# Linear attention and a swish layer on one core: a hand-ordered kernel with one chunk per batch, row tiles and DMA transposes

## The chip, the cores and the metric

The kernel runs on one core of a Trainium2 chip. A core has five engines with queues of their own: PE (TensorE, matmuls; PEld is its weight load), DVE (VectorE), ACT (ScalarE), POOL (GpSimd) and SP (SyncE, which here only issues DMAs). The metric is the device time of one execution in microseconds. Each engine works through its own instructions in order; where one needs what another engine made, it waits on a semaphore, and everything behind it on its engine waits too.

## What is computed

A linear attention over 8 batches and 8 heads, 576 tokens of 64 numbers each, gives x, one row of 512 numbers a token. Then comes a two-layer network with a swish in the middle.

```
q, k, v: (8, 8, 576, 64) float32; w_in (512, 2048); w_out (2048, 512); beta (2048)

q_s = exp(q - max(q, axis=-1));  q_s = q_s / (sum(q_s, axis=-1) + 1e-09)
k_s = exp(k - max(k, axis=2));   k_s = k_s / (sum(k_s, axis=2) + 1e-09)
kv  = einsum('bhsd,bhse->bhde', k_s, v)
att = einsum('bhsd,bhde->bhse', q_s, kv)
x   = att.transpose(0, 2, 1, 3).reshape(4608, 512)
h   = x @ w_in
g   = h * (1.0 / (1.0 + exp(-beta * h)))
out = g @ w_out
```

The softmax of q runs over the 64 numbers of a token, that of k over the 576 tokens of a head. Inputs and output are float32 in HBM; both kernels multiply in bf16. Both also write the swish as h/2 * (1 + tanh(beta h/2)), with the half folded into the cast of w_out.

## The kernel before

A scheduling layer (a tile framework) takes the program as written and puts each engine's instructions in an order of its own, by dependences and free buffers. So attention of one batch, and matmuls of another, stand mixed on PE.

`attention(b)` (called for b = 0 to 7) works on one batch in five pieces of tokens, 128, 128, 128, 128 and 64 rows. For every piece it loads q on SP's queue (L109), k on POOL's (L115) and v on POOL's, cast to bf16 on the way (L121). A row of a head is 64 float32, so each packet is 256 bytes. ACT takes exp of q (L129) and of k (L146), without subtracting a maximum. DVE sums q over each head (L131), takes the reciprocal (L135) and multiplies (L137). Then, for each of four pairs of heads, PE adds up kvE over the five pieces (L157); a column of ones beside v gives the sum over k, and DVE divides by it (L167 to L173). PE transposes the normalised q of the pair against an identity (L179), DVE copies the result out of PSUM (L185), and PE multiplies q by kv, two 64 x 64 tiles of the array at once (L193, L199). ACT copies x, transposed, into `xT` (L205). `xT` is cut into nine chunks of 512 tokens, which don't fall together with the batches of 576.

`mlp_A(c)` goes over 16 blocks of 128 hidden features of one chunk: four matmuls of 512 columns (L213) into a PSUM bank, tanh on ACT (L221), one DVE operation that makes g (L225). `mlp_B(c)` makes four output blocks of 128 tokens, 16 matmuls of 512 columns each (L241), a copy on ACT (L249) and a store on SP's queue (L251). There are 576 matmuls of either kind.

The weights come in twelve loads on SP's queue (L74, L80) behind the first q loads, and DVE casts them to bf16 (L86, L90). The main loop calls attention of batch b, then `mlp_A` of chunk b and `mlp_B` of chunk b - 1.

Of the kernel before, what the change touches and what calls it, by code (L numbers as in the profile page):

```python
# [12 lines left out]
ACTF = mybir.ActivationFunctionType  # L13


@with_exitstack
def kernel(
# [10 lines left out]
    nc = tc.nc  # L28
# [5 lines left out]
    NTOK = B * S  # L34
    KT = DM // P
    NJ = FF // P
    CHUNK = 512
    NCH = NTOK // CHUNK
    assert NTOK % CHUNK == 0
    S_CHUNKS = [(0, 128), (128, 128), (256, 128), (384, 128), (512, 64)]  # L40
    NSC = len(S_CHUNKS)
    HP = H // 2

    const = ctx.enter_context(tc.tile_pool(name="const", bufs=1))
    wst = ctx.enter_context(tc.tile_pool(name="wstage", bufs=2))
    stage = ctx.enter_context(tc.tile_pool(name="stage", bufs=3))
    atn = ctx.enter_context(tc.tile_pool(name="atn", bufs=2))
    xtp = ctx.enter_context(tc.tile_pool(name="xt", bufs=1))
    gt = ctx.enter_context(tc.tile_pool(name="gt", bufs=2 * NJ))
    outp = ctx.enter_context(tc.tile_pool(name="outp", bufs=2))  # L50
    psA = ctx.enter_context(tc.tile_pool(name="psA", bufs=1, space=bass.MemoryType.PSUM))
    psM = ctx.enter_context(tc.tile_pool(name="psM", bufs=2, space=bass.MemoryType.PSUM))

    identity = const.tile([P, P], BF16, name="identity")
    make_identity(nc, identity[:])

    beta_t = const.tile([P, NJ], F32, name="beta_t")
    nc.sync.dma_start(beta_t[:], moe_beta.rearrange("(j p) -> p j", p=P))
    beta_half = const.tile([P, NJ], F32, name="beta_half")
    nc.vector.tensor_single_scalar(beta_half[:], beta_t[:], 0.5, ALU.mult)  # L60

    w_in_b = const.tile([P, KT, FF], BF16, name="w_in_b")
    w_out_b = const.tile([P, NJ, DM], BF16, name="w_out_b")
    w_in_dram = moe_w_in.rearrange("(kt p) f -> p kt f", p=P)
    w_out_dram = moe_w_out.rearrange("(j p) f -> p j f", p=P)

    w_stage_in = []
    w_stage_out = []

    def issue_weight_dmas():  # L70
        for i in range(2 * KT):
            kt, half = divmod(i, 2)
            t = wst.tile([P, FF // 2], F32, tag="wst_in", bufs=4, name=f"w_in_st{i}")
            nc.sync.dma_start(  # L74
                t[:], w_in_dram[:, kt, half * (FF // 2) : (half + 1) * (FF // 2)]
            )
            w_stage_in.append(t)
        for jj in range(NJ // 4):
            t = wst.tile([P, 4, DM], F32, tag="wst_out", bufs=2, name=f"w_out_st{jj}")
            nc.sync.dma_start(t[:], w_out_dram[:, 4 * jj : 4 * jj + 4, :])  # L80
            w_stage_out.append(t)

    def cast_weights():
        for i in range(2 * KT):
            kt, half = divmod(i, 2)
            nc.vector.tensor_copy(  # L86
                w_in_b[:, kt, half * (FF // 2) : (half + 1) * (FF // 2)], w_stage_in[i][:]
            )
        for jj in range(NJ // 4):
            nc.vector.tensor_single_scalar(  # L90
                w_out_b[:, 4 * jj : 4 * jj + 4, :], w_stage_out[jj][:], 0.5, ALU.mult
            )

    xT = [xtp.tile([P, KT, CHUNK], BF16, name=f"xT{c}") for c in range(NCH)]

    gT_chunks: dict[int, list] = {}

    STAGE_BUFS = 3
    ATN_DEEP = 2 * NSC

    def attention(b: int):
        Ek = []
        qs = []
        vaug = []
        q_st = []
        k_st = []
        for ci, (s0, rows) in enumerate(S_CHUNKS):
            qt = stage.tile([P, H, D], F32, tag="q_st", bufs=NSC)
            nc.sync.dma_start(  # L109
                qt[:rows], q[b, :, s0 : s0 + rows, :].rearrange("h p d -> p h d")  # L110
            )
            q_st.append(qt)
        for ci, (s0, rows) in enumerate(S_CHUNKS):
            kt_ = stage.tile([P, H, D], F32, tag="k_st", bufs=NSC)
            nc.gpsimd.dma_start(  # L115
                kt_[:rows], k[b, :, s0 : s0 + rows, :].rearrange("h p d -> p h d")
            )
            k_st.append(kt_)
        for ci, (s0, rows) in enumerate(S_CHUNKS):
            vt = atn.tile([P, H, D + 1], BF16, tag="vaug", bufs=ATN_DEEP)  # L120
            nc.gpsimd.dma_start(  # L121
                vt[:rows, :, 0:D], v[b, :, s0 : s0 + rows, :].rearrange("h p d -> p h d")
            )
            vaug.append(vt)

        for ci, (s0, rows) in enumerate(S_CHUNKS):
            nc.vector.memset(vaug[ci][:rows, :, D : D + 1], 1.0)  # L127
            Eq = atn.tile([P, H, D], BF16, tag="Eq")
            nc.scalar.activation(Eq[:rows], q_st[ci][:rows], ACTF.Exp)  # L129
            qz = atn.tile([P, H], F32, tag="qz")  # L130
            nc.vector.tensor_reduce(  # L131
                qz[:rows], Eq[:rows], axis=mybir.AxisListType.X, op=ALU.add
            )
            rqz = atn.tile([P, H], F32, tag="rqz")
            nc.vector.reciprocal(rqz[:rows], qz[:rows])  # L135
            qst = atn.tile([P, H, D], BF16, tag="qs", bufs=ATN_DEEP)
            nc.vector.tensor_tensor(  # L137
                qst[:rows],
                Eq[:rows],
                rqz[:rows].unsqueeze(2).to_broadcast((rows, H, D)),  # L140
                ALU.mult,
            )
            qs.append(qst)

            Ekt = atn.tile([P, H * D], BF16, tag="Ek", bufs=ATN_DEEP)
            nc.scalar.activation(  # L146
                Ekt[:rows, :],
                k_st[ci][:rows].rearrange("p h d -> p (h d)"),
                ACTF.Exp,
            )  # L150
            Ek.append(Ekt)

        col_abs = b * S
        for j in range(HP):
            kvE = psA.tile([P, 2 * (D + 1)], F32, tag="kvE")
            for ci, (s0, rows) in enumerate(S_CHUNKS):
                nc.tensor.matmul(  # L157
                    kvE[:, :],
                    Ek[ci][:rows, ds(P * j, P)],
                    vaug[ci][:rows].rearrange("p h e -> p (h e)")[  # L160
                        :rows, ds(2 * j * (D + 1), 2 * (D + 1))
                    ],
                    start=(ci == 0),
                    stop=(ci == NSC - 1),
                )
            rkz = atn.tile([P, 1], F32, tag="rkz")
            nc.vector.reciprocal(rkz[0:D, :], kvE[0:D, D : D + 1])  # L167
            nc.vector.reciprocal(rkz[D:P, :], kvE[D:P, 2 * D + 1 : 2 * D + 2])
            kvp = atn.tile([P, D], BF16, tag="kvp")
            nc.vector.tensor_scalar(  # L170
                kvp[0:D, :], kvE[0:D, 0:D], rkz[0:D, :], None, op0=ALU.mult
            )
            nc.vector.tensor_scalar(  # L173
                kvp[D:P, :], kvE[D:P, D + 1 : 2 * D + 1], rkz[D:P, :], None, op0=ALU.mult
            )

            qsT_ps = psA.tile([P, S], BF16, tag="qsT_ps", bufs=2)
            for ci, (s0, rows) in enumerate(S_CHUNKS):
                nc.tensor.transpose(  # L179
                    qsT_ps[:, s0 : s0 + rows],  # L180
                    qs[ci][:rows].rearrange("p h d -> p (h d)")[:rows, ds(j * P, P)],
                    identity[:rows, :rows],
                )
            qsT = atn.tile([P, S], BF16, tag="qsT")
            nc.vector.tensor_copy(qsT[:, :], qsT_ps[:, :])  # L185

            s_done = 0
            while s_done < S:
                c = (col_abs + s_done) // CHUNK
                off = (col_abs + s_done) % CHUNK  # L190
                w = min(CHUNK - off, S - s_done)
                xps = psA.tile([P, CHUNK], F32, tag="xps")
                nc.tensor.matmul(  # L193
                    xps[0:D, 0:w],
                    kvp[0:D, :],
                    qsT[0:D, s_done : s_done + w],
                    tile_position=(0, 0),
                )
                nc.tensor.matmul(  # L199
                    xps[D:P, 0:w],  # L200
                    kvp[D:P, :],
                    qsT[D:P, s_done : s_done + w],
                    tile_position=(64, 64),
                )
                nc.scalar.copy(xT[c][:, j, off : off + w], xps[:, 0:w])  # L205
                s_done += w
# [90 lines left out]
```

## Time and profile before

| | us |
|---|---|
| median of 3 runs | 369.32 |
| lowest and highest run | 367.2, 369.77 |
| span of the profiled execution | 366.7 |
| PE busy, DVE busy | 317.5, 207.0 |
| ACT busy, POOL busy | 185.2, 69.3 |

The profile comes from one execution, whose span runs from its first to its last instruction. The table of busy times says how full an engine is over the whole span; since the kernel has a start, a loop and an end with different limits, stretches of the span are looked at by themselves. The "chain of waits" goes back from the last instruction to what released it at each step. In the lists of instructions, a line is that of the kernel's text, `out<-in` are the program's names, `128x512` are partitions and elements, and x is a count. A row's last part is the idle time of the engine ahead of these instructions, and what ended it. In the row of the granted clock a digit is tenths of full speed in one of 40 equal slices of the span. The mean granted clock of the execution is 0.980.

DMA moved 41.72 MB in 88486 packets, of which 78480 were under 512 bytes. Of the loads, q tiles of 256 KB took 5.4 us from issue to landing (median), and the stores of 256 KB 2.0 us.

### The profile page before, as it was taken

To read this page: it belongs to the slowest core of one execution; us is meant where nothing else is said; L and a number is where in the kernel's file an instruction comes from. 1 tells how busy PE (TensorE), PEld (TensorE's weight loads), DVE (VectorE), ACT (ScalarE), POOL (GpSimd) and SP (SyncE) were. 2 spreads that over 40 slices of the span, in tenths; PEclk is the share of its full clock that TensorE was granted. 3 is DMA by queue.
4 is the path that set the end of the run, shared out by engine and by line. 5 is a ranking of instruction groups with operands and counts; after the bars stand their busy time and mean duration, and the time that the engine had idled before them with its cause. 6 is when DMAs were issued, how large, how long until landed. Compare 5 with 4: busy or idle time off the path is not lost.

```text
span 366.7 us, 4552 instructions
## 1 busy us (share of the span) xinstructions
PE 317.5 (87%) x1570; PEld 139.3 (38%) x1600; DVE 207.0 (56%) x477; ACT 185.2 (50%) x325; POOL 69.3 (19%) x86
## 2 busy tenths in 40 slices
PE   0125669899998999899989998999999999999995
PEld 0011223443433444344433443345344444444442
DVE  1554736988988937664767566654452545255100
ACT  3312426768668745755485538552554355355211
POOL 8281433035017001800090004000000000000000
PEclk9999768999999999999999999999999999999999
DMA  8999999649719802950293019001001000100111
GB/s 187 250 356 327 266 254 241 160 103 219 204 46 188 221 31 78 182 150 27 62 179 115 2 57 93 30 0 57 27 3 57 32 29 2 57 29 29 59 67 76
DMA packets 88486, 41.72 MB, mean 114 GB/s; under 512 B 78480, under 2 KB 78480, under 8 KB 88464
## 3 DMA queue, kind: packets, MB, share of 16 engines
q0 software_dynamic: 40448, 14.16, 28.8%
q1 hardware_dynamic: 48016, 27.28, 26.3%
q8 instruction: 12, 0.20, 0.2%
q14 instruction: 10, 0.08, 0.1%
HBM read 36.71 MB, written 9.44 MB: 126 GB/s over the span
## 4 chain that ended last, share of the span: by engine, by line
PE 67%; DMA 12%; DVE 11%; issue 4%; ACT 3%; SPq 2%; POOL 1%; ACTq 0%; POOLq 0%
PE hT L213 30%; PE acc L241 27%; DMA qt<-in_q_dram 6%; DMA vt<-in_v_dram 4%; PE kvE L157 4%; PE qsT_ps L179 3%; DVE g L225 3%; PE xps L193 3%; DMA w_in_st_311<-in_moe_w_in_dram 3%; DVE qst L137 2%; SPq L109 2%; DVE qz L131 2%; ACT th L221 1%; DVE w_in_b L86 1%; DVE qsT L185 1%
## 5 line engine op out<-in xcount | busy, mean ns | idle before, releaser
L241 PE MATMUL acc<-w_out_b,g 128*128 128x512 bf16 x561 | 143.8, 381 | 0.6 <-DVE g L225 0.2
L221 ACT ACTIVATE th<-hT,beta_half 128x512 bf16<-128x512 f32 x144 | 97.8, 686 | 72.4 <-PE hT L213 68.8
L225 DVE SCALAR_TENSOR_TENSOR g<-th,hT 128x512 bf16<-128x512 bf16 x144 | 97.7, 685 | 64.8 <-ACT th L221 64.4
L213 PEld LDWEIGHTS <-w_in_b 128*128 128x128 bf16 x576 | 54.4, 98 | 87.3 <-issue 34.4
L241 PEld LDWEIGHTS <-g 128*128 128x128 bf16 x576 | 54.9, 98 | 63.8 <-issue 0.9
L121 POOL DMA_DIRECT2D vt<-in_v_dram x40 | 33.9, 871 | 121.6 <-DVE qz L131 101.8
L249 ACT COPY o_sb<-acc 128x512 f32<-128x512 f32 x36 | 21.0, 584 | 44.6 <-PE acc L241 41.1
L179 PE MATMUL qsT_ps<-identity,qst 128*128 128x128 bf16 (+1 forms) x160 | 18.8, 226 | 19.1 <-DVE qst L137 17.8
L131 DVE TENSOR_REDUCE qz<-Eq 128x8 f32<-128x512 bf16 (+1 forms) x40 | 26.8, 671 | 13.3 <-ACT Eq L129 8.7
L129 ACT ACTIVATE Eq<-qt 128x512 bf16<-128x512 f32 (+1 forms) x40 | 25.0, 627 | 11.0 <-DMA qt<-in_q_dram 8.5
L137 DVE TENSOR_TENSOR qst<-Eq,rqz 128x512 bf16<-128x512 bf16 (+1 forms) x40 | 27.1, 684 | 2.6 <-DVE rqz L135 1.9
L157 PE MATMUL kvE<-vt,Ekt 128*128 128x130 bf16 (+1 forms) x160 | 20.9, 232 | 7.8 <-DVE vt L127 7.2
L213 PE MATMUL hT<-xT_93,w_in_b 128*128 128x512 bf16 x63 | 20.7, 469 | 6.0 <-DVE g L225 5.8
L193 PE MATMUL xps<-qsT,kvp 64*64 64x512 bf16 (+7 forms) x64 | 20.2, 316 | 3.9 <-DVE kvp L170 2.6
L179 PEld LDWEIGHTS <-qst 128*128 128x128 bf16 (+1 forms) x160 | 11.1, 99 | 27.3 <-DVE qst L137 19.6
L199 PE MATMUL xps<-qsT,kvp 64*64 64x512 bf16 (+7 forms) x64 | 20.3, 317 | 0.3 <-issue 0.3
L167 DVE RECIPROCAL rkz<-kvE 64x1 f32<-64x1 f32 x32 | 5.0, 158 | 27.3 <-PE kvE L157 26.5
L157 PEld LDWEIGHTS <-Ekt 128*128 128x128 bf16 (+1 forms) x160 | 12.4, 100 | 19.6 <-issue 10.7
L213 PE MATMUL hT<-xT_96,w_in_b 128*128 128x512 bf16 x63 | 16.4, 378 | 2.0 <-DVE g L225 2.0
L213 PE MATMUL hT<-xT_97,w_in_b 128*128 128x512 bf16 x63 | 16.5, 378 | 1.6 <-DVE g L225 1.6
L213 PE MATMUL hT<-xT_94,w_in_b 128*128 128x512 bf16 x62 | 16.4, 380 | 0.9 <-DVE g L225 0.8
L213 PE MATMUL hT<-xT_95,w_in_b 128*128 128x512 bf16 x62 | 16.2, 379 | 1.1 <-DVE g L225 0.9
(121 smaller groups left out, 222.7 us busy)
## 6 DMA issues: line engine op xcount, KB each, us to landing
out_dram<-o_sb SPq DMA_DIRECT2D x36, 256.0 KB, 2.0
qt<-in_q_dram SPq DMA_DIRECT2D x32, 256.0 KB, 5.4
vt<-in_v_dram POOLq DMA_DIRECT2D x32, 128.0 KB, 5.6
qt<-in_q_dram SPq DMA_DIRECT2D x8, 128.0 KB, 6.1
w_out_st_315<-in_moe_w_out_dram SPq DMA_DIRECT2D x1, 1024.0 KB, 12.0
w_out_st_317<-in_moe_w_out_dram SPq DMA_DIRECT2D x1, 1024.0 KB, 14.9
w_out_st_319<-in_moe_w_out_dram SPq DMA_DIRECT2D x1, 1024.0 KB, 10.7
w_out_st_321<-in_moe_w_out_dram SPq DMA_DIRECT2D x1, 1024.0 KB, 11.8
```

The costliest lines, as they stand in the source:

```text
L121: nc.gpsimd.dma_start(vt[:rows, :, 0:D], v[b, :, s0 : s0 + rows, :].rearrange("h p d -> p h d"))
L129: nc.scalar.activation(Eq[:rows], q_st[ci][:rows], ACTF.Exp)
L131: nc.vector.tensor_reduce(qz[:rows], Eq[:rows], axis=mybir.AxisListType.X, op=ALU.add)
L137: nc.vector.tensor_tensor(qst[:rows], Eq[:rows], rqz[:rows].unsqueeze(2).to_broadcast((rows, H, D)), ALU.mult,)
L157: nc.tensor.matmul(kvE[:, :], Ek[ci][:rows, ds(P * j, P)], vaug[ci][:rows].rearrange("p h e -> p (h e)")[:rows, ds(2 * j * (D + 1), 2 * (D ...
L179: nc.tensor.transpose(qsT_ps[:, s0 : s0 + rows], qs[ci][:rows].rearrange("p h d -> p (h d)")[:rows, ds(j * P, P)], identity[:rows, :rows],)
L193: nc.tensor.matmul(xps[0:D, 0:w], kvp[0:D, :], qsT[0:D, s_done : s_done + w], tile_position=(0, 0),)
L213: nc.tensor.matmul(hT[:, :], w_in_b[:, kt, ds(j * P, P)], xT[c][:, kt, :], start=(kt == 0), stop=(kt == KT - 1),)
L221: nc.scalar.activation(th[:, :], hT[:, :], ACTF.Tanh, scale=beta_half[:, j : j + 1])
L225: nc.vector.scalar_tensor_tensor(out=g[:, :], in0=th[:, :], scalar=1.0, in1=hT[:, :], op0=ALU.add, op1=ALU.mult,)
L241: nc.tensor.matmul(acc[:, :], gts[j][:, ds(st * P, P)], w_out_b[:, j, :], start=(j == 0), stop=(j == NJ - 1),)
L249: nc.scalar.copy(o_sb[:, :], acc[:, :])
```

## The change

The kernel is written anew, and the order of every engine's instructions is the order in which the program names them (`manual_schedule`).

- A chunk is one batch of 576 tokens. A token row p * 9 + t of a batch lies on partition p (of 64) at place t (of 9), so a load moves 9 x 64 float32, 2304 bytes, per head and partition. Heads 0 to 3 lie on partitions 0 to 63 and heads 4 to 7 on 64 to 127. All loads of q, k and v of later batches are issued on SP; in batch 0 half of them on ACT.
- Maxima are taken as in the reference: of q over 64 numbers (`q_max`, DVE), of k over a head's 576 tokens (`k_max`, `k_small`, DVE: a reduce over 9 strided places, then a transposed reduce over partitions and a transpose back). The subtractions are on POOL (one of batch 0 on DVE), and so is the division of q from batch 1 on.
- `kv_mm` adds up kv over 9 places in two row tiles of 64 partitions, 36 matmuls of 130 columns a batch. `x_mm` uses all four 64 x 64 quadrants of the array, 16 matmuls of 320 or 256 columns a batch; to that end the odd w_in row blocks are loaded with their halves exchanged.
- q is transposed by DMA on SP's queue (`q_xbar`), in two pieces; in batch 0 by PE.
- `unit` is one block of 128 hidden features: 8 matmuls of 288 columns into two PSUM banks, a tanh and a g of 576 columns. There are three such pairs of banks (`big`), which attention uses too, and two single banks for output blocks.
- An output block is still 128 tokens and 16 matmuls of 512 columns; an odd batch's first block takes the last 64 rows of the batch before and its own first 64. Of a batch's blocks, two or three (`n_alone`) stand by themselves around the next batch's `kv_mm` and `x_mm`; the rest go, one or more matmuls at a time, between the units of the next batch.
- `attn_stream(nb)` is the attention work of the next batch on DVE, ACT, POOL and SP, one step after each unit. For batch 1 these steps stand after all units of batch 0, beside the output blocks of batch 0.
- 24 matmuls on zeros come first on PE, and 8 more ahead of batch 0's `kv_mm`.

The diff, cut to its core:

```diff
+    ctx.enter_context(tc.manual_schedule())
+    psA = ctx.enter_context(tc.tile_pool(name="psA", bufs=3, space=bass.MemoryType.PSUM))
+    psB = ctx.enter_context(tc.tile_pool(name="psB", bufs=2, space=bass.MemoryType.PSUM))
...
+    def load(eng, dst, src, b, hh, h0, h1, t0, t1):
+        s = src[b, 4 * hh + h0 : 4 * hh + h1].rearrange("h (p t) d -> p h t d", p=PR)
+        d = dst[PR * hh : PR * hh + PR, h0:h1, t0:t1, :].rearrange("p h t d -> p h (t d)")
+        eng.dma_start(d, s[:, :, t0:t1, :].rearrange("p h t d -> p h (t d)"))
...
+    def k_max(jj):
+        nc.vector.tensor_reduce(
+            km[:, 2 * jj * D : (2 * jj + 2) * D].rearrange("p (h d) -> p h d", h=2),
+            Kf[:, 2 * jj : 2 * jj + 2].rearrange("p h t d -> p h d t"),
+            axis=AX.X, op=ALU.max)
+    def k_small(j0, j1):
+        c = slice(4 * j0, 4 * j1)
+        nc.vector.tensor_reduce(kr[:, c], ..., axis=AX.X, op=ALU.max, apply_transpose=True)
+        for g in range(4):
+            o = g ^ 1
+            nc.vector.tensor_copy(kw[32 * g : 32 * g + 32, c], kr[32 * o : 32 * o + 32, c])
+        nc.vector.tensor_tensor(kM[:, c], kr[:, c], kw[:, c], ALU.max)
+        nc.vector.transpose(MB[:, 2 * j0 : 2 * j1, :]..., kM[:, c].unsqueeze(2)...)
+    def k_sub(eng, jj):
+        x = Kf[:, 2 * jj : 2 * jj + 2]
+        m = MB[:, 2 * jj : 2 * jj + 2, :].unsqueeze(2).to_broadcast((P, 2, NT, D))
+        eng.tensor_tensor(x, x, m, ALU.subtract)
...
+    def q_norm(eng, t0, t1):
+        eng.tensor_tensor(qs[:, t0:t1]..., Eq[:, :, t0:t1, :], rq[:, :, t0:t1]..., ALU.mult)
+    def q_xbar(t0, t1):
+        nc.sync.dma_start_transpose(
+            qT[:, 2 * t0 : 2 * t1, :], qs[:, t0:t1].rearrange("p t h d -> p (t h d)"))
...
+    def kv_mm(jj):
+        if jj == 0:
+            kvps[0] = big()
+        for t in range(NT):
+            for hh in range(2):
+                nc.tensor.matmul(
+                    kvps[0][:, 512 * hh + 130 * jj : 512 * hh + 130 * jj + 130],
+                    Ek[PR * hh : PR * hh + PR, t, 2 * jj : 2 * jj + 2, :]...,
+                    va[PR * hh : PR * hh + PR, t, jj, :],
+                    start=(t == 0), stop=(t == NT - 1))
...
+    def x_mm(hh):
+        ps = [big(), big()]
+        for t0, t1 in ((0, 5), (5, 9)):
+            for jj in range(2):
+                for i in range(2):
+                    o = i ^ jj
+                    nc.tensor.matmul(
+                        ps[jj][PR * o : PR * o + PR, 192 + PR * t0 : 192 + PR * t1],
+                        kvs[PR * i : PR * i + PR, hh, jj, :], qT[...])
...
+    def unit(b, j, kts=(0, 1, 2, 3)):
+        h = big()
+        for n, kt in enumerate(kts):
+            for a in range(2):
+                nc.tensor.matmul(h[:, 224 + 288 * a : 512 + 288 * a], w_in_b[:, kt, j, :],
+                    xT[b % 2][:, kt, 288 * a : 288 * a + 288], ...)
+        nc.scalar.activation(th[:], hv, ACTF.Tanh, scale=beta_h[:, j : j + 1])
+        nc.vector.scalar_tensor_tensor(out=G[j][...], in0=th[:], scalar=1.0, in1=hv, ...)
...
+    def attn_stream(nb, pe):
+        def steps():
+            k_max(0)
+            yield
+            k_max(1)
+            yield
+            k_small(0, 2)
+            k_sub(nc.gpsimd, 0)
+            k_sub(nc.gpsimd, 1)
+            yield
+            q_max(0, 5)
+            q_sub(nc.gpsimd, 0, 5)
+            yield
+            q_max(5, NT)
+            q_sub(nc.gpsimd, 5, NT)
+            yield
+            k_exp(0)
+            yield
+            v_cast(nc.vector, 0)
+            k_exp(1)
+            if nb + 1 < B:
+                load2(Kf, k, nb + 1, 0, 4, 0, NT)
+            yield
+            v_cast(nc.vector, 1)
+            if nb + 1 < B:
+                load2(Vf, v, nb + 1, 0, 4, 0, NT)
+            yield
+            q_exp(0, 5)
+            yield
+            q_sum(0, 5)
+            q_norm(nc.gpsimd, 0, 5)
+            q_exp(5, NT)
+            if nb + 1 < B:
+                load2(Qf, q, nb + 1, 0, 4, 0, NT)
+            yield
+            q_sum(5, NT)
+            q_norm(nc.gpsimd, 5, NT)
+            q_xbar(0, 5)
+            yield
+            q_xbar(5, NT)
+            yield
...
+    for j in range(NJ):
+        unit(0, j)
...
+    s = attn_stream(1, None)
+    for j in range(NJ):
+        for x in blocks:
+            x.step(1)
+        advance(s)
+    advance(s, 99)
+    kv_mm(0)
+    kv_mm(1)
+    kv_norm()
+    for hh in range(2):
+        ps = x_mm(hh)
+        x_out(1, hh, ps, [nc.scalar, nc.vector])
+    pending = []
+    for b in range(1, B):
...
+        for j in range(NJ):
+            unit(b, j)
+            for _ in range(n_mixed):
...
+                if pending:
+                    pending[0].step(1)
+            advance(s)
...
+        n_alone = {1: 3}.get(b, 2)
+        alone, pending = main[:n_alone], main[n_alone:]
+        alone[0].step(NJ)
+        kv_mm(0)
+        kv_mm(1)
+        kv_norm()
+        for x in alone[1:-1]:
+            x.step(NJ)
+        alone[-1].step(6)
+        ps = x_mm(0)
+        x_out(b + 1, 0, ps, [nc.scalar, nc.vector])
+        alone[-1].step(5)
+        ps = x_mm(1)
+        x_out(b + 1, 1, ps, [nc.scalar, nc.vector])
+        alone[-1].step(5)
```

## The prediction

> **What bounds the kernel now.** All of it is reckoned in one profiled execution: span 366.7 us, against a median of 369.3 us for the runs, so 2.6 us lie around the span. First the page's busy times and granted clock, then two stretches of the late loop, each one batch long.
>
> ```profile
> PE 317.5 (87%) x1570; PEld 139.3 (38%) x1600; DVE 207.0 (56%) x477; ACT 185.2 (50%) x325; POOL 69.3 (19%) x86
> ...
> PEclk9999768999999999999999999999999999999999
> ```
>
> ```profile
> 213.43:250.64 37.21, 35.20 (x183) 15.73 (x187) 22.18 (x52) 20.42 (x37) 4.21 (x5) 1.00 0.33 44
> 250.64:285.67 35.03, 34.73 (x181) 15.56 (x186) 16.23 (x36) 16.13 (x29) 0.00 (x0) 1.00 0.08 31
> ```
>
> After the length of a stretch come PE, PEld, DVE, ACT and POOL busy, clock, DMA share and GB/s. The second batch is PE from end to end: 34.73 of 35.03 us. The chain of waits (start, us, what) says what PE is paid for, and what stands before that:
>
> ```profile
> 6.58 9.80 DMA qt<-in_q_dram
> ...
> 21.76 9.27 DMA w_in_st_311<-in_moe_w_in_dram
> ...
> 245.29 4.96 PE acc L241 x23
> ...
> 354.13 8.60 PE acc L241 x39
> ```
>
> 23 matmuls of 512 columns take 4.96 us, 0.2157 each. A late batch issues 128 of them, 27.6 us; the other 7.4 us are attention on PE: 20 transposes, 20 kvE and 16 xps matmuls with the waits among them. Two loads hold the start, and an unbroken run of L213 begins only at 44.2 us. PE ends at 362.7, so the tail is 4.0 us. Start, attention on PE and tail are what can be won. Rows that price the rest (count | busy us, mean ns | idle before):
>
> ```profile
> L225 DVE SCALAR_TENSOR_TENSOR g<-th,hT 128x512 bf16<-128x512 bf16 x144 | 97.7, 685 | 64.8 <-ACT th L221 64.4
> ...
> L137 DVE TENSOR_TENSOR qst<-Eq,rqz 128x512 bf16<-128x512 bf16 x32 | 21.6, 686 | 2.3 <-DVE rqz L135 1.9
> L131 DVE TENSOR_REDUCE qz<-Eq 128x8 f32<-128x512 bf16 x32 | 21.5, 676 | 9.3 <-ACT Eq L129 8.1 <-ACT th L221 0.8 <-issue 0.3
> ...
> L129 ACT ACTIVATE Eq<-qt 128x512 bf16<-128x512 f32 x32 | 20.0, 627 | 8.6 <-DMA qt<-in_q_dram 6.4 <-DVE qst L137 1.4 <-ACT th L221 0.6
> ...
> masks.py:199 POOL TENSOR_SCALAR_AFFINE_SELECT identity<-identity 128x128 bf16<-128x128 bf16 x1 | 0.3, 311 | 0.1
> ```
>
> **PE after the change.** A token costs the same in `unit` (L287): 288 columns are 0.121 us by proportion, a unit of 8 matmuls 0.97, the 16 units of a batch 15.5. An output block is 16 x 0.2157 = 3.45 us; there are 36, as before. Transposes leave PE except in batch 0. `kv_mm` has 36 matmuls of 130 columns. The timeline of PE has four of that width:
>
> ```profile
> 290.98 0.40 PE L157 MATMUL kvE<-vt,Ekt 128*128 128x130 bf16 x4
> ```
>
> One alone lasts 0.23, so they start 0.057 apart: 2.05 us for 36, half of it if the two halves of the array overlap. `x_mm` has 16 matmuls of 288 columns on average; L193 and L199 now start at the same moment in pairs, so 8 x 0.121 = 0.97 us. Attention on PE: 3.0 us a batch instead of 7.4.
>
> **DVE and ACT.** Two L225 back to back take 1.28 us, so the second adds 0.60; an 8-element MEMSET takes 0.065; that leaves 1.05 ns an element. Reduces and two-input operations of 1152, 1280, 1024 elements are then 1.34, 1.48, 1.21 us, 0.08 less back to back; g at 576 is 0.75, or 0.66. Exp is 0.20 us + 0.83 ns an element (ACT copies of 64 and 448 columns take 213 and 532 ns): 1.16, 1.26, 1.05. Casts of 576 are 0.36 back to back (0.69 at 1024 elements, 1.23 at 2048). Within a stretch of units DVE gets for the next batch's attention: maxima of k 2.52, the small chain (L152) 1.3, maxima of q 2.53, casts of v 1.44, sums and reciprocals of q 3.13; together 10.9 us.
>
> **POOL.** It loses the load issues (0.87 to 1.1 us each) and gets `k_sub`, `q_sub`, `q_norm`: 6912 elements a batch in six instructions. No such operation is in the trace. From above, 311 ns for 128 elements with nothing taken off is 2.4 ns; from below, DVE's 1.05. I take 1.65, the same row less 0.10 for an almost empty MEMSET on POOL, because it is POOL's own: 2.0, 2.2 and 1.8 us an instruction.
> [...]
>
> POOL and DVE also meet. In the timeline of DVE the second of these casts lies beside POOL's load issues:
>
> ```profile
> 17.84 0.69 DVE L86 CAST w_in_b<-w_in_st_299 128x1024 bf16<-128x1024 f32 x1
> ...
> 19.28 1.13 DVE L86 CAST w_in_b<-w_in_st_301 128x1024 bf16<-128x1024 f32 x1
> ```
>
> It is 0.43 us longer. I charge that to each of four casts of v, 1.7 us a batch (ends: nothing, and 8 us if each sits out a POOL instruction).
> [...]
>
> **Queues.** k and v loads go from POOL's queue to SP's, at 0.43 us an issue (a w_in load of 128 packets now). SP's loads for the next batch wait on exps and casts, its transposes on POOL; stores stand behind them and the three osb buffers cover that. 3.5 MB in 33 us is 107 GB/s, where early slices show 250 to 356: hidden.
>
> **Start.** The first k tile is now used 4.5 us after issue; with more bytes ahead of it I put k at 5.0. On DVE: maximum and small chain 7.7; second maximum, chain and DVE's own `k_sub` 11.7; maximum of q 13.2; POOL 15.5; exp 16.8; sum 18.5; norm 20.0; `kv_norm` 21.0; second part of q: maximum 22.2, POOL 24.2, exp 25.3, sum 26.8, norm 28.1; transposes and copy 1.4, `x_mm` and xT 2.0 with semaphores: **32**. The 16 units go at (0.97 + 2.1 for tanh, g and semaphores) / 3 = 1.02 us with three PSUM pairs, 16.4; 1.7 to the last g; 1.5 for a low clock at first (7, 6, 8 tenths at 37 to 64 us in the row above): **51.6**.
>
> **Batch 1's attention is uncovered.** It stands behind all units of batch 0 on DVE. From 51.6: w_out cast 1.2, maxima 2.7, chain 1.3, POOL 4.0 and 2.2 (at 11.4), exp and sum 14.4, `q_norm` twice on POOL 18.4, DMA transpose, `x_mm` and xT 1.5. The transpose has no row: a 256 KB store lands in 2.0 us, a 256 KB load in 5.4; I take 3.5, between the two. Sum 23.4: batch 1's units start at **75.0**. PE has only 13.8 us of blocks and 2 of `kv_mm` in there. In later stretches the sums end 21.9 us in and POOL's last norm at 23.7, while `x_mm` is due at 32.2 (below), so 8.5 us of transposing are hidden; of a longer transpose each us costs seven, one in each batch.
>
> **Batches 1 to 7.** PE alone: units 7 x 15.5, 32 blocks 110.4, six attentions 18.0, tail 3.5 (the last copy halved): **240.4**. Then DVE: unit 14 needs the PSUM that g 11 frees, and DVE is there 2.1 (to the first g) + 12 x 0.66 + 10.9 + 1.7 = 22.6 us into the stretch. PE alone starts unit 14 at 14 x (0.97 + 0.43) = 19.6 with two blocks mixed in, at 22.6 with three, at 13.6 with none. Stalls: 3.0 in batches 2, 3, 5, none in 4, 6, 9.0 in batch 1, and 0.7 at six transitions for `kv_norm` and xT: **22.2**.
> 75.0 + 240.4 + 22.2 = 337.6, and 2.6: **340 us**; this case alone 328 to 352, chance 0.45.
>
> **Rivals.** (1) Slower: the POOL chain takes PE's place. ACT's exps wait for POOL with tanhs of later units queued behind, and `x_mm` for the transposes. `x_mm` is due 25.4 + 3.45 + 2.05 + 1.3 = 32.2 us into the stretch; POOL and transpose are done at 7.9 + 0.6 + 6.9r + 3.5, late from r = 2.9 ns an element. Up to there only start and batch 1 pay, 9.2 us per ns, 11.5; beyond, six batches too, 50.6 per ns. The 29 us of gain are gone at 3.3 ns; at 4 it is 407. For it: no POOL row of this shape. Against: 2.4 was the row's upper end. 0.22. (2) A smaller gain: DVE is longer, because the strided maxima of k run at half rate (2.7 a stretch and in batch 1, 16 to 19), or two casts a batch each sit out a POOL instruction of 2.0 us (3.1 above my charge, 19): 354 to 359 with one, 375 with both. 0.21. (3) More gain: DVE stays under PE (no 18 of stalls), POOL at DVE's rate (0.6 ns less, 5.5): 316 to 328. 0.12.
>
> **Numbers.** 340 is the first case's. The range from 318 to 378 leaves out the lower end of (3) and most of (1) above its turning point. One per cent (365.6 to 373) is about what can be told from no change: 0.08, out of (2)'s upper and (1)'s lower edge. (2) is otherwise faster: 0.45 + 0.12 + 0.13 = 0.70. Slower 0.22.
>
> **What would show it.** Units from 32 and batch 1's from 75 us; kvE spacing at most 0.06; POOL's 1152-element subtraction 2.0 us (over 3.8 is rival 1); PE's idle time in mixed stretches ended by DVE's g, not by ACT behind POOL; casts of v under 0.9 us; maxima of k 1.3 us, not 2.6. I am wrong if PE idles over 8 us in a batch from 2 on, or if the transposes land after `x_mm` is due.

## The result and the profile after

The changed kernel takes 390.68 us (median of 4 runs, 389.72 to 391.38) against 368.94 us for the kernel before on the same chip (4 runs): 1.060 times as long, 95% interval 1.056 to 1.064. That is 51 us above the forecast of 340 and outside its range of 318 to 378. The profiled execution has a span of 389.6 us.

Lines of its page: the engines' busy times, then the granted clock and the share of time that the DMA engines were moving data, in tenths, in 40 slices of the span.

```profile
PE 302.7 (78%) x2066; PEld 175.8 (45%) x2066; DVE 232.7 (60%) x334; ACT 162.8 (42%) x219; POOL 128.5 (33%) x61
...
PEclk9665999855999999999999699989998799999999
DMA  7989992697059812991099415981099211621132
```

PE is now busy for 78% of the span, 87% before. The clock, which before was down at the start alone, is down again and again: the late dips (6, 8, then 8 and 7) stand in or just behind slices in which the DMA row is at 9. So the late loop is no longer PE from end to end. The stretches from one batch's first unit to the next one's show where it stands (length, then PE, PEld, DVE, ACT and POOL busy, clock, DMA share, GB/s):

```profile
37.90:93.10 55.20, 34.23 (x244) 20.79 (x243) 29.45 (x41) 21.05 (x28) 27.42 (x10) 0.81 0.84 196
...
135.20:177.40 42.20, 34.83 (x246) 20.22 (x245) 27.48 (x40) 19.05 (x26) 13.57 (x6) 0.96 0.58 124
177.40:220.90 43.50, 35.76 (x245) 20.39 (x244) 27.49 (x40) 19.04 (x26) 13.58 (x6) 0.92 0.57 120
220.90:263.40 42.50, 37.85 (x261) 21.79 (x260) 27.40 (x40) 19.59 (x27) 13.58 (x6) 0.96 0.61 129
...
306.90:344.30 37.40, 36.16 (x262) 21.39 (x261) 27.39 (x40) 19.60 (x27) 13.59 (x6) 1.00 0.28 52
```

The stretches from 135.2 and 177.4 us do the same work and take 42.2 and 43.5 us. Those from 220.9 and 306.9 us have one output block more, 16 matmuls, and take 42.5 and 37.4. What sets the last apart is that no loads of a later batch are in it (52 GB/s instead of 120 to 129), and its clock is full. The groups of instructions name the wait (count | busy us, mean ns of one | idle before, and what ended it):

```profile
L301 DVE SCALAR_TENSOR_TENSOR G<-th,big 128x576 bf16<-128x576 bf16 x128 | 93.9, 743 | 45.3 <-ACT th L300 44.5
L175 POOL TENSOR_TENSOR Kf<-Kf,MB 128x1152 f32<-128x1152 f32 x15 | 39.1, 2625 | 172.6 <-issue 104.6
...
L273 PE MATMUL big<-qT,kvs 64*64 64x320 bf16 (+1 forms) x128 | 11.7, 385 | 36.7 <-DMA qT<-qs 34.5
...
L145 DVE TENSOR_REDUCE km<-Kf 128x128 f32<-128x1152 f32 x16 | 33.9, 2125 | 4.9 <-DMA Kf<-in_k_dram 4.8
...
L127 DVE CAST va<-Vf 128x576 bf16<-128x576 f32 x30 | 21.0, 744 | 0.0
```

PE waits 34.5 us for transposed q: 19.3 of it in batch 1, where nothing covers the attention, and 15.2 in batches 2 to 6. POOL's subtraction is 2.63 us, far from the 3.8 of the slower rival. The maxima of k are 2.13 us, not 1.34. SP's queue shows the transposes themselves, in a stretch with loads and in the last one without (start, time that SP spent on issuing, what):

```profile
151.62 1.37 SPq L91 DMA_DIRECT2D Kf<-in_k_dram  x2
154.38 1.36 SPq L91 DMA_DIRECT2D Vf<-in_v_dram  x2
156.11 1.25 SPq L91 DMA_DIRECT2D Qf<-in_q_dram  x2
160.20 10.57 SPq L213 DMA_TRANSPOSE qT<-qs  x2
```

```profile
331.67 3.10 SPq L213 DMA_TRANSPOSE qT<-qs  x2
```

The two issues take 10.57 us behind six loads and 3.10 us without. A transpose lands 9.0 us after its issue in the median, 3.0 at least, 13.0 at most; the step in the prediction was 3.5. On PE the wait and what follows it look so:

```profile
172.12 0.33 PE L273 MATMUL big<-qT,kvs 64*64 64x320 bf16 x4 [2.69 <-DMA qT<-qs]
172.90 0.30 PE L273 MATMUL big<-qT,kvs 64*64 64x256 bf16 x4 [0.45 <-DMA qT<-qs]
173.13 2.09 PE L336 MATMUL acc<-w_out_b,G 128*128 128x512 bf16 x5
```

Five matmuls of 512 columns take 2.09 us right behind the wait. The same five take 1.25 at the end of the last stretch, where no wait is:

```profile
341.62 1.25 PE L336 MATMUL acc<-w_out_b,G 128*128 128x512 bf16 x5
```

In steps of 1 us the granted clock is 1.00 up to 173 us, 0.50 to 0.70 from 173 to 177, and 1.00 again. So a wait of 3.1 us costs more than itself.

Against the prediction's own sum (the third and fourth columns are two of the experiments that follow):

| us, from the profiled executions | forecast | after | e5 | e9 |
|---|---|---|---|---|
| first unit starts | 32 | 37.9 | 37.9 | 35.3 |
| from there to batch 1's first unit | 43.0 | 55.2 | 49.1 | 46.1 |
| from there to the end of the span | 262.6 | 296.5 | 274.3 | 266.2 |
| span | 337.6 | 389.6 | 361.3 | 347.6 |

The forecast is 52.0 us short: 5.9 in the start, 12.2 up to batch 1, 33.9 after that.

### The profile page after: what moved, and what is told of

Its sections match the earlier page's. It is cut to its first block, busy times and chain, and to the rows that moved or that the text cites. A ratio compares the mean times of both kernels' runs of the same rounds, so it can differ in the third digit from the quotient of the medians.

```text
span 389.6 us, 5329 instructions
## 1 busy us (share of the span) xinstructions
PE 302.7 (78%) x2066; PEld 175.8 (45%) x2066; DVE 232.7 (60%) x334; ACT 162.8 (42%) x219; POOL 128.5 (33%) x61
## 5 line engine op out<-in xcount | busy, mean ns | idle before, releaser
L291 PE MATMUL big<-xT,w_in_b 128*128 128x288 bf16 x1024 | 146.4, 291 | 23.9 <-DVE G L301 23.3
L336 PE MATMUL acc<-w_out_b,G 128*128 128x512 bf16 x544 | 145.2, 393 | 0.0
L291 PEld LDWEIGHTS <-w_in_b 128*128 128x128 bf16 x1024 | 101.6, 99 | 77.6 <-issue 37.3
L300 ACT ACTIVATE th<-big,beta_h 128x576 bf16<-128x576 f32 x128 | 94.0, 740 | 66.5 <-PE big L291 64.5
L301 DVE SCALAR_TENSOR_TENSOR G<-th,big 128x576 bf16<-128x576 bf16 x128 | 93.9, 743 | 45.3 <-ACT th L300 44.5
L175 POOL TENSOR_TENSOR Kf<-Kf,MB 128x1152 f32<-128x1152 f32 x15 | 39.1, 2625 | 172.6 <-issue 104.6
L336 PEld LDWEIGHTS <-G 128*128 128x128 bf16 x576 | 56.0, 100 | 52.5 <-issue 8.6
L273 PE MATMUL big<-qT,kvs 64*64 64x320 bf16 (+1 forms) x128 | 11.7, 385 | 36.7 <-DMA qT<-qs 34.5
L195 POOL TENSOR_TENSOR Qf<-Qf,qm 128x1280 f32<-128x1280 f32 (+1 forms) x16 | 33.7, 2130 | 10.9 <-DMA wi<-in_moe_w_in_dram 10.9
L145 DVE TENSOR_REDUCE km<-Kf 128x128 f32<-128x1152 f32 x16 | 33.9, 2125 | 4.9 <-DMA Kf<-in_k_dram 4.8
L205 POOL TENSOR_TENSOR qs<-Eq,rq 128x1280 bf16<-128x1280 bf16 (+1 forms) x14 | 29.5, 2124 | 20.3 <-DVE rq L202 20.3
## 6 DMA issues: line engine op xcount, KB each, us to landing
Qf<-in_q_dram SPq DMA_DIRECT2D x14, 576.0 KB, 13.2
```

The source lines that it names most:

```text
L145: nc.vector.tensor_reduce(km[:, 2 * jj * D : (2 * jj + 2) * D].rearrange("p (h d) -> p h d", h=2), Kf[:, 2 * jj : 2 * jj + 2].rearrange("p ...
L175: eng.tensor_tensor(x, x, m, ALU.subtract)
L195: eng.tensor_tensor(x, x, m, ALU.subtract)
L205: eng.tensor_tensor(qs[:, t0:t1].rearrange("p t h d -> p h t d"), Eq[:, :, t0:t1, :], rq[:, :, t0:t1].unsqueeze(3).to_broadcast((P, 4, t1 ...
L291: nc.tensor.matmul(h[:, 224 + 288 * a : 512 + 288 * a], w_in_b[:, kt, j, :], xT[b % 2][:, kt, 288 * a : 288 * a + 288], start=(n == 0), st ...
L300: nc.scalar.activation(th[:], hv, ACTF.Tanh, scale=beta_h[:, j : j + 1])
```

## The experiments

All times are medians of four runs. Each kernel is the changed one with the edit shown; the kernel before took 367.8 to 368.9 us beside them.

**e1: the loads of the next batch behind the transposes.**

```diff
             v_cast(nc.vector, 0)
             k_exp(1)
-            if nb + 1 < B:
-                load2(Kf, k, nb + 1, 0, 4, 0, NT)
...
             q_xbar(5, NT)
+            if nb + 1 < B:
+                load2(Kf, k, nb + 1, 0, 4, 0, NT)
+                load2(Qf, q, nb + 1, 0, 4, 0, NT)
+                load2(Vf, v, nb + 1, 0, 4, 0, NT)
```

> All loads of the next batch stand behind both DMA transposes on SP's queue. Theory A (the transposes are slow because 3.5 MB of loads are queued just ahead of them): the two issues take 3.1 us together instead of 10.6 to 11.9, the pieces land in 3 to 5 us, x_mm waits for less than 1 us from batch 2 on and about 11 us less in batch 1, the clock stays near 1.00 in the late stretches, and the time is 355 to 365. Rival B (a transpose of this size takes 9 us by itself): issue and landing stay as they are and the time is 387 to 393. Either way the next k lands late: if DVE's first maximum of k waits for it by more than 3 us a batch, some of the gain is lost, and the time is 365 to 375.

Measured: 376.1 us. The transposes are what theory A says: 3.4 us to landing in the median, two issues 3.95 us, no wait of `x_mm` from batch 2 on, late stretches of 37.2 us at a clock of 1.00. The forecast's 3.5 us was right for a transpose with no loads ahead of it. But the time is 11 us above A's range. ACT's timeline in batch 1 has the reason:

```profile
99.13 0.58 ACT L125 COPY osb<-big 128x512 f32<-128x512 f32 x1 [23.66 <-DMA out_dram<-osb]
```

ACT's fourth copy of batch 0's output blocks needs one of three osb buffers; the store that frees it stood behind transposes and loads on SP, and x of batch 1 stood behind that copy on ACT. Batch 1's units began at 100.4 us instead of 93.1. Over the whole run the 70 stores of 128 KB landed in 7.4 us (median); in e5, where batch 0's stand ahead of the loads, in 2.4. So it is not transposes alone that are slow behind loads.

**e5: in batch 1 SP issues stores, transposes, loads, in that order** (the steps of the next batch stop after the tenth while batch 0's output blocks run, so that the stores are named first, and the loads of batch 2 are named last; e1's edit otherwise).

```diff
-        advance(s)
+        if j < 10:
+            advance(s)
     advance(s, 99)
+    load2(Kf, k, 2, 0, 4, 0, NT)
+    load2(Qf, q, 2, 0, 4, 0, NT)
+    load2(Vf, v, 2, 0, 4, 0, NT)
```

> As e1_loads_behind, and in batch 1 SP's order is: stores of batch 0's blocks, transposes, loads of batch 2. In e1 x_mm of batch 1 stood 16.6 us still because ACT's fourth copy into osb waited 23.7 us for a store that was queued behind six loads. Theory A (order on SP's queue is all that was wrong with the DMAs): batch 1's units start at 83 to 85 instead of 101 us, the late stretches stay at 37.2 us, the time is 357 to 362. Rival: the loads of batch 2, now behind stores and transposes, land after batch 2's first maximum is due, and half of the gain is lost: 366 to 370.

Measured: 361.6 us, 0.981 of the kernel before (0.976 to 0.986): 29 us less than the changed kernel, by the order of DMA issues alone. The late stretches:

```profile
166.00:203.20 37.20, 32.96 (x246) 19.80 (x245) 27.49 (x40) 19.04 (x26) 13.58 (x6) 1.00 0.64 140
```

Set beside the stretch of 43.5 us above, which has the same work: 6.3 us less. The waits for q were 3.5 of them (3.2 and 0.3). PE's busy time was 35.76 at a clock of 0.92 and is 32.96 at 1.00; 32.96 / 0.92 is 35.8, so the other 2.8 us are the same matmuls at the lower clock. The loads by themselves do not lower it: the DMA share is 0.64 here, at a clock of 1.00. In batch 1 `x_mm` still waits 12.8 us for q, since nothing covers the attention there.

**e6 and e13: the same loads at the same places, issued by ACT, or by POOL.** They ask whether the transposes are slow because they stand behind the loads in one queue, or because the DMA engines are busy with the loads' bytes.

```diff
-                load2(Kf, k, nb + 1, 0, 4, 0, NT)
+                load2(Kf, k, nb + 1, 0, 4, 0, NT, nc.scalar, nc.scalar)
...
```

> The loads of the next batch are issued by ACT at the same places in the program, the transposes and stores stay on SP. If order within one queue is what slows the transposes: issue 3.1 us for two, landing under 5 us, x_mm waits under 1 us from batch 2 on, time 356 to 368 (some 4 us of issuing a batch on ACT, which has room). If it is that the DMA engines are busy with the loads' bytes whichever queue brought them: issue and landing stay near 11 and 9 us, x_mm waits 3 us a batch, time 386 to 393.

Measured: 395.2 us, above both ranges; transposes landing in 7.2 us (median), two issues 5.77 and 5.28 us for batches 2 and 3. The transposes lie between the two theories, because the stretches themselves changed: on ACT a load's issue waits for DVE's cast or for the exp, tanhs stand behind it, and the stretches grew to 42.4 us without any wait of `x_mm` from batch 2 on. These stretches settle little. Batch 1 says more: there the loads go out 2 to 8 us ahead of the transposes, 1 to 7 in the changed kernel, but on ACT's queue, and the first piece lands 11.2 us behind its issue and `x_mm` waits 19.3, against 13.0 and 19.3.

> As e6_loads_act, but POOL issues the loads of the next batch, at the same places, so that no tanh stands behind them. If the transposes are slow because the 16 DMA engines are still moving the loads' bytes, whatever queue they came by: two transposes stay long (SP's issue over 6 us, landing 7 us or more), and the time is 385 to 400. If it is that they stand behind the loads in one queue: landing under 4.5 us, x_mm waits under 1 us from batch 2 on, and the time is 358 to 372, some of it lost to the six issues a batch that POOL now has between its divisions.

Measured: 408.8 us. POOL issues the loads, and SP, on a queue without any load, sits on the transposes. POOL's and SP's timelines:

```profile
117.33 1.23 POOL L91 DMA_DIRECT2D Vf<-in_v_dram  x2
...
121.44 1.25 POOL L91 DMA_DIRECT2D Qf<-in_q_dram  x2
```

```profile
121.53 14.02 SPq L213 DMA_TRANSPOSE qT<-qs  x2
```

14.02 us for two issues, 12.7 to landing, 49.1 us of waits at `x_mm`. So it is not the order within one queue: transposes issued while 3.5 MB of loads are under way are slow whichever queue brought the loads. Its time is above both ranges, on the side of the busy DMA engines.

**e2: q transposed by PE in every batch**, as in batch 0 (18 matmuls against the identity around `kv_mm`, copies on DVE and ACT, no DMA transposes).

```diff
-            q_xbar(0, 5)
...
         alone[0].step(NJ)
+        take = q_pe(0, 5)
+        take(nc.vector, 0, 5)
+        take(nc.scalar, 5, 10)
         kv_mm(0)
         kv_mm(1)
+        take = q_pe(5, NT)
+        take(nc.vector, 0, 4)
+        take(nc.scalar, 4, 8)
```

> From batch 1 on q is transposed by PE against the identity, as in batch 0, beside kv_mm; there are no DMA transposes. PE gets 18 matmuls of 128 columns a batch (about 1.1 us), DVE and ACT one or two copies each (0.7 us apiece). Both A and B expect no wait of x_mm for a DMA: 15 us of waits from batch 2 on, some 10 us of low clock and about 11 us of batch 1 go, 7 x 2 us come back: 365 to 372. If instead the time stays above 383, the transposes were not what held x_mm; the sums or POOL's division would be next.

Measured: 376.6 us, 4.6 above the range. Its late stretches take 38.5 to 38.7 us, 1.3 to 1.4 more than e5's: that is what 18 transposes and their copies cost where a hidden DMA costs nothing. Moving q by DMA is right there, if the loads are kept out of its way. Of the 15 us between e2 and e5, 8.8 lie in batch 1 (57.9 us against 49.1): the stores of batch 0 still stand behind the loads of batch 2, ACT waits 13.9 us for one of them, and PE's second group of transposes 9.9 us for ACT. That is why the time is above the range.

**e3: the first reduce of k over neighbouring numbers.**

```diff
-            Kf[:, 2 * jj : 2 * jj + 2].rearrange("p h t d -> p h d t"),
+            Kf[:, 2 * jj : 2 * jj + 2].rearrange("p h t d -> p h (t d)").rearrange("p h (d t) -> p h d t", t=NT),
```

> The first reduce of k reads nine neighbouring numbers instead of nine places 64 apart; sizes are the same, what it gives is not the maximum over tokens. Stride theory: 1.34 us each instead of 2.13; 1.6 us less at the start and in batch 1, and 1.6 us in each of five stretches if DVE sets the end of the units there: 379 to 383; if the transposes alone set when x_mm starts, the same 1.6 us, since the whole chain starts sooner. If the stretches have slack, only start and batch 1 pay: 386 to 388. Rival: the length is that of the operation (1.85 ns an element whatever the order): 2.1 us each and 389 to 392.

Measured: 379.6 us, 11.1 less, as the stride theory has it. The group of the reduce in this kernel:

```profile
L145 DVE TENSOR_REDUCE km<-Kf 128x128 f32<-128x1152 f32 x16 | 21.4, 1344 | 4.6 <-DMA Kf<-in_k_dram 4.6
```

1.344 us against 2.125 for the same 1152 numbers taken 64 apart. `x_mm` still waits 32.7 us for transposes; the chain has only moved forward, by 1.0 us at batch 0's first unit and 11.5 at batch 7's, 1.5 us a batch.

**e7: DVE kept clear of POOL's long casts in the start.**

```diff
-    q_norm(nc.vector, 5, NT)
-    cast_w_in(nc.gpsimd, 1)
+    q_norm(nc.gpsimd, 5, NT)
+    cast_w_in(nc.scalar, 1)
...
     v_cast(nc.vector, 1)
+    nc.vector.tensor_single_scalar(beta_h[:], beta_t[:], 0.5, ALU.mult)
     q_exp(0, 5)
```

> Start only: the second q_norm moves to POOL ahead of its casts of w_in, the first of those casts (1024 elements) goes to ACT, beta_h is computed before the first sum of q. So DVE does nothing beside POOL's long casts. If POOL's casts hold DVE up (3.20 us for q_norm, 2.24 us for beta_h, against 1.2 and 0.2 by size): first unit at 33 to 35 us instead of 37.9, time 386.5 to 388. If the two were long for another reason and POOL's division takes as much: first unit at 37 to 38.5 us, time 390 to 392.

What it is about, from the timeline of the changed kernel, POOL's casts of w_in and DVE beside them:

```profile
27.54 13.37 POOL L127 CAST w_in_b<-wi 128x1024 bf16<-128x1024 f32 x4
...
30.26 3.20 DVE L205 TENSOR_TENSOR qs<-Eq,rq 128x1024 bf16<-128x1024 bf16 x1
...
34.92 2.24 DVE L407 TENSOR_SCALAR beta_h<-beta_t 128x16 f32<-128x16 f32 x1
```

Sixteen numbers take 2.24 us, and 1024 take 3.20, where the same instruction takes 1.23 in e8 (below), beside an idle POOL. Measured in e7: 388.0 us, first unit at 36.2 instead of 37.9. The time is in the expected range, the place is not: the first unit came forward by 1.7 us, not 3 to 5. POOL's division takes 1.91 us, so 1.3 of the 3.20 go. beta_h gave little, about the other 0.4: while DVE was on it, PE and ACT were still making x.

**e9: e5, e3 and e7 together.**

> e5_stores_first, e3_kmax_contig and e7_start together (the first reduce of k reads neighbours, so what it gives is not the maximum over tokens). If the three causes add up: 390.7 - 29.1 - 11.1 - 2.7 = 348, with late stretches of 35.5 us in place of 37.2 and batch 1's units from about 80 us. If they share the same us (a shorter DVE chain only uncovers the next wait): 354 to 358.

Measured: 349.8 us, 0.948 of the kernel before (0.944 to 0.952). The causes add up. A late stretch of it:

```profile
121.70:157.30 35.60, 32.51 (x240) 19.79 (x244) 25.92 (x40) 19.05 (x26) 13.58 (x6) 1.00 0.60 132
```

35.6 us, where the forecast had 36.0 (36.5 with an output block more, measured 35.8 and 37.9). (What e3's reduce gives is still one number for all tokens of a head and column, so the softmax of k is the same function; it is no longer shifted by the exact maximum.)

**e10: the exact maximum of k by pairwise maxima**, with e5 and e7.

```diff
+        nc.vector.tensor_tensor(kt[:, h0:h1], x[:, :, 0:4], x[:, :, 4:8], ALU.max)
...
+        nc.vector.tensor_tensor(y[:, :, 0:2], y[:, :, 0:2], y[:, :, 2:4], ALU.max)
+        nc.vector.tensor_tensor(m, y[:, :, 0], y[:, :, 1], ALU.max)
+        nc.vector.tensor_tensor(m, m, Kf[:, h0:h1, 8], ALU.max)
```

> As e9, but with the true maximum of k, taken by four pairwise maxima over neighbouring runs of 64 (1024 + 512 + 256 + 256 numbers for all heads) instead of one strided reduce. By DVE's 1.05 ns a number that is 2.5 us a batch instead of 4.25, 0.2 less than with the reduce over neighbours: 346 to 350. If operations of two float32 inputs that stride over heads are slower than that, 352 to 358.

Measured: 352.2 us, in the second range of the expectation, but for another reason. The late stretches are nearly as short as e9's (35.8 us); the 2 us are lost in the start, where the first unit comes at 37.5, 2.2 later than e9's. DVE's timeline there:

```profile
9.07 0.69 DVE L151 TENSOR_TENSOR kt<-Kf 128x512 f32<-128x512 f32 x1
9.80 2.71 DVE L156 TENSOR_TENSOR kt<-kt 128x256 f32<-128x256 f32 x1
```

256 numbers take 2.71 us beside POOL's first subtraction; the same instruction took 0.42 us before POOL had begun.

**e12: casts of v into a dense tile**, on e5 (the attention then uses constants in place of v).

```diff
-            cast(eng, va[:, :, jj, c : c + D], Vf[:, 2 * jj + i])
+            cast(eng, vc[:], Vf[:, 2 * jj + i])
```

> e5_stores_first with the casts of v written into a dense tile instead of runs of 64 every 260 (the matmuls then read constants in place of v). If the strided output costs the casts of v their speed: 0.44 us each as the dense casts of 1024 (0.69) suggest, instead of 0.744; 1.2 us a stretch less on DVE, 352 to 355. If it is the input or the size: 0.74 us each and 360 to 363.

Measured: 371.8 us, 10 more than e5, which neither theory had. The shortest cast took 0.452 us, as the first theory says; the median took 1.50 and the longest 2.77. DVE and POOL in one stretch:

```profile
146.14 2.96 DVE L128 CAST vc<-Vf 128x576 bf16<-128x576 f32 x2
...
149.69 1.99 DVE L128 CAST vc<-Vf 128x576 bf16<-128x576 f32 x2
```

```profile
141.00 5.21 POOL L176 TENSOR_TENSOR Kf<-Kf,MB 128x1152 f32<-128x1152 f32 x2 [23.57 <-DMA out_dram<-osb]
146.16 4.72 POOL L196 TENSOR_TENSOR Qf<-Qf,qm 128x1280 f32<-128x1280 f32 x2
```

The dense casts are long beside POOL's instructions: the four of batch 1 take 8.07 us together, to 74.56 us, beside four subtractions of which the last ends at 74.24. POOL's second pair takes 4.72 us instead of the 4.21 that it takes in the changed kernel. The strided casts of the changed kernel take 0.744 us beside the same subtractions (0.742 to 0.747 over all 30), two in a row 1.41; in e8, with POOL idle beside them, two in a row take 1.41 as well (from 126.68 us).

Set side by side: the cast takes 0.744 us in the strided form and 0.452 at its shortest in the dense one, but 1.50 (median) and up to 2.77 in this kernel. Two operations with two inputs are long beside POOL too: 2.71 us instead of 0.42 (e10's pairwise maximum) and 3.20 instead of 1.23 (the division). Why one form of the cast is longer there and the other is not, no run here shows.

**e4, e8 and e11: no maxima and no subtractions**, as in the kernel before (the softmax is the same function of q and k). e4 leaves out `k_max`, `k_small`, `k_sub`, `q_max` and `q_sub`; e8 adds e5's order, e11 adds e7's start.

> All maxima and subtractions are left out (exp of q and k as they come, as before the change). DVE loses 4.3 + 1.3 + 2.7 us a batch, POOL 9.5. Expected: about 10 us less at the start, 12 to 14 in batch 1; in the stretches the units are no longer held by DVE (3 to 5 us each) and the divisions come some 10 us sooner, so that the transposes, however long, are done before x_mm is due: another 30 to 40. Time 325 to 340. If x_mm still waits for transposes from batch 2 on, the loads move ahead with the exps and the transposes stay behind them: 345 to 360.

> All maxima and subtractions left out as in e4_no_max, and SP's order as in e5_stores_first. e4 still waited 27.3 us at x_mm for transposes, 13.7 of it in batch 1, and lost some 8 us to the lower clock behind those waits. Expected: no such wait from batch 2 on, 8 to 10 us less in batch 1, the stretches at 33.5 us (PE alone): 325 to 333. If loads behind the transposes come too late once the stretches are short: 338 to 345, with DVE or ACT waiting for k, v or q.

> e8_no_max_order (all maxima and subtractions left out) with the start of e7. In e8 beta_h takes 3.55 us of DVE beside POOL's cast of w_in, and x_mm's copy of the second half waits for it: 1.5 to 2.5 us less, 330 to 331. No change (332 to 333) if the loads of w_in hold the start there.

Measured: 352.5, 332.5 and 332.9 us. In e4 the loads moved ahead together with the exps, the transposes stayed behind them, and `x_mm` waited 27.3 us: the second case of its expectation, not the first. With the order mended, 20.0 us go, and e8 is 0.902 of the kernel before (0.898 to 0.907), the best of all. Against e5 it shows what maxima and subtractions cost with the order mended: 29.1 us. A late stretch of e8 is PE from end to end again:

```profile
115.30:147.80 32.50, 31.97 (x245) 19.84 (x244) 19.56 (x29) 18.80 (x26) 4.21 (x2) 1.00 0.66 146
```

e11's start gives nothing: its first unit is at 31.8 us, e8's at 32.0, though beta_h no longer takes 3.55 us there. PE's timeline in e11 has the reason:

```profile
27.84 1.03 PE L224 MATMUL big<-ident,qs 128*128 128x128 bf16 x8 [5.87 <-POOL qs L205]
28.80 0.48 PE L273 MATMUL big<-qT,kvs 64*64 64x320 bf16 x4
```

`x_mm` begins at 28.80 us, in e8 at 27.25: the division takes 1.91 us on POOL, 1.23 in e8 on DVE beside an idle POOL, and the chain ahead of it runs 0.75 us later. Together these use up the 1.68 us that PE waited for DVE's copy of x, behind beta_h, in e8.

## Why the prediction was wrong

**The step that failed is "the transpose has no row ... I take 3.5", with "8.5 us of transposing are hidden".** The price was a choice between two rows of other DMAs, one number for any traffic. It happens to hold where no loads are ahead: 3.4 us in e1 and e5. But the change issues next batch's loads 3 to 9 us ahead of the transposes, and I set those loads down as "107 GB/s ... hidden", an average that says nothing of when they are under way: in the stretch shown from 151.6 us to the landing of q, 13.2 us (median) behind its issue at 156.1. Beside them the two transposes took 10.6 to 11.9 us. The rest of the chain was nearly right: in the stretch from 135.2 us the transposes are issued 25.0 us in, where I had 23.7, and `x_mm` was ready but for q at 34.2, where I had 32.2. So there were 9.2 us to hide them in, 8.5 in my sum; the first piece landed 11.8 us behind its issue. The consequence that I wrote down, that `x_mm` goes late and each further us costs every batch, is what happened.

Order of issue alone is worth 390.7 - 361.6 = 29.1 us, 28.3 between the profiled executions: 6.1 of batch 1 (55.2 to 49.1), 15.2 of waits of 1.4 to 3.8 us ahead of five batches' `x_mm`, and 7.0 that are left for the lower clock behind them, which I had nowhere in the loop. The order of stores, which I waved through ("the three osb buffers cover that"), was a trap as well: in the changed kernel ACT's fourth copy already waited 16.3 us for a store behind the transposes.

**The maxima of k, "1.34 each", are 2.13.** The proportion by elements holds for neighbouring numbers (1.344, and 1.47 and 1.21 for the maxima of q), and not for a stride. Rival 2 had this cause with "half rate" and 16 to 19 us; the runs show 1.6 times as long and 11.1 us. Its second half, casts that sit out POOL's instructions, did not happen in the changed kernel (0.742 to 0.747 us each); in e12 casts of another form are longer beside them (four in 8.07 us).

**The casts of v: sum right, reason wrong.** 0.36 and a charge of 0.43 for POOL made 0.79; it is 0.744 beside POOL, and two in a row take 1.41 us beside it and beside an idle POOL (e8). That the sum was close is luck.

**The start, "32", was 37.9.** The first k is used 1.0 us later than I had (5.97), the two strided maxima cost 1.6, DVE's division beside POOL's casts another 2.0. e7 and e3 give back 1.7 and 1.0 of it, e9 2.6 together. Of the rest, POOL's longer instructions are part.

**Rival 1 had the right wait and the wrong price.** It let `x_mm` wait for the transposes, but only if POOL went over 2.9 ns a number. POOL's instructions take 2.63, 2.34 and 1.91 us, where I had 2.0, 2.2 and 1.8: 2.28 ns a number for k and 1.83 to 1.87 for q, where I had 1.65 and 0.10 us. Six of them are 13.6 us a batch, not 12.0, and that was not what decided.

**What held:** units of 0.98 us, output blocks of 3.45, tanh and g 0.74 each, DVE as the engine behind PE's idle time in mixed stretches. L291 waits 23.3 us for g: 8.4 in batch 1, 4.2 in each of batches 2, 3 and 5, and 1.1 in 4 and 6, where I had 9.0, 3.0 and none; in e9, 7.6, 2.8 to 3.0, and 0.2 and 2.0. `kv_mm` took 1.20 us, not 2.05, near the half that the sum left open. With the three mis-sized terms put back, e9 stands at 347.6 us of span against 337.6: 3.3 of the 10 lie in the start, 3.1 up to batch 1, and 3.6, net, in seven batches. What makes up these 10 was not tried further.

## What to carry to other kernels

Take a DMA's price from the traffic in which it will run (a transpose took 3.4 us with no loads ahead, 9.0 in the changed kernel, in the median): before a transfer that someone waits for, look at what else is on the DMA engines at that time, and issue prefetches behind it, not ahead, also when they have a queue of their own (12.7 us with the loads on POOL's). Give every transfer on a shared queue its due time, stores too, for they hold the buffers that the next copies need (23.7 us of ACT's wait in e1). And price a DVE operation by its access pattern, not only its number of elements: a stride (2.125 us against 1.344), a dense form of a cast (0.452 at its shortest against 0.744), and a POOL instruction beside it (2.71 against 0.42) each moved a cost here, by 1.6 to 6.5 times.

## What the hardware showed that was not expected

- Transposes of 256 to 320 KB land in 3.4 us (median) with no loads ahead, in 6.5 to 13.0 us with loads ahead on their own queue, and in 12.7 us (median, 15.3 at most) with the same loads on POOL's queue. SP is held meanwhile: 2.8 to 4.0 us for two issues, 10.6 to 11.9, and 13.0 to 14.0.
- Behind a wait of some 3 us on PE the granted clock is down for about 4 us (0.50 to 0.70 from 173 to 177 us), 0.92 to 0.96 over the stretch: 2.8 us on top of 3.5 us of waiting in the stretch from 177.4 us. The late stretches of e5, without the wait, stand at 1.00.
- A faster form of a cast (0.452 us instead of 0.744) made the kernel 10 us slower: beside POOL's instructions four of them take 8.07 us, and the median is 1.50.
- A reduce over nine numbers 64 apart takes 2.13 us for 1152 numbers, over neighbours 1.34.
